# Splitting each weight load of an attention and channel-mix kernel into 120 and 8 partitions

## The chip, the cores and the metric

The kernel runs on one core of one Trainium2 chip. The metric is device time in microseconds (us): the median of 3 runs before the change was 168.54 us (168.08 to 169.32). The core has a matrix engine (TensorE, PE in the profile, with PEld for its weight loads), VectorE (DVE), ScalarE (ACT), GpSimd (POOL) and SyncE (SP). In this kernel SP issues nearly all transfers between the main memory (HBM) and the on-chip memory (SBUF, 128 partitions); the transfers themselves run on 16 DMA engines.

## The reference

The inputs are q, k and v (4 batches, 8 heads, 768 positions, head dimension 64) and the weights of a channel mix. All are float32.

```python
scores = scale * np.matmul(q, k.transpose(0, 1, 3, 2))
keep = is_sink | in_window        # first 4 positions, or the last 128
scores = np.where(keep, scores, -1000000000.0)
a = np.exp(scores - np.max(scores, axis=-1, keepdims=True))
a = a / (np.sum(a, axis=-1, keepdims=True) + 1e-09)
x = np.matmul(a, v)               # -> (4, 768, 512), heads side by side
...
x_prev = x shifted by one position
xk = mu_k * x + (1.0 - mu_k) * x_prev
xr = mu_r * x + (1.0 - mu_r) * x_prev
k = np.maximum(xk @ w_k, 0.0)     # w_k: 512 x 1024
v = k * k @ w_v                   # w_v: 1024 x 512
r = 1.0 / (1.0 + np.exp(-(xr @ w_r)))   # w_r: 512 x 512
out = r * v
```

## The kernel before

The work is cut into 12 units: four batches of three blocks of 256 positions. For each unit the kernel loads k, q and v, casts them to bfloat16, turns k and q so that the head dimension lies on the partitions (on TensorE, or with a transposing transfer in later units), forms the scores of the window and of the sinks, takes the exponential on ScalarE, masks on VectorE, multiplies with v on TensorE and divides (`attend`). `mix` then turns the result and forms xk and xr, and `ffn` does the three products with the weights. The `ffn` of a unit runs beside the attention of the next one.

Nothing is scheduled on the chip. Every step is an operation of a plan (`P.op`), and a list written out by hand, `ORDER`, gives the order in which the operations are emitted; `CHOICE` says which engine takes a step that several could do, `SLOTS` which buffer each tile gets. Negative entries of `ORDER` are matmuls on a tile of zeros (L1014) that keep TensorE running, most of them before real work is there. Each engine runs its own instructions in that order, and waits are set by the data and the buffers. The costs that stand in the calls of `P.op` (600.0, `service`, `descs`) are left from the search for the order and do nothing at run time.

The weights are loaded in five pieces of 1 MB each by `load_weight`: the two halves of w_k (`wka`, `wkb`), `wr`, and the two halves of w_v (`wva`, `wvb`). Each piece goes into one of three float32 buffers of the pool `w32` with 128 partitions of 4 x 512 values, that is four runs of 2 KB per partition. `cast` (L492 and on) then makes bfloat16 copies, on ScalarE (L498) or VectorE (L502, L504): `wk_sb`, `wr_sb`, `wv_h`. The pieces wva and wvb take the buffers of wka and wkb, so their transfers wait for the casts of those.

All these transfers are issued by SP, in the order of `ORDER`, between the loads of k, q and v (L304, L314, L334). Around the weights the order is: a v and a q load, wka, a k load, wkb, a k load, the two v loads of the second unit, one v load of the third, wr, wva, wvb, and then loads of the third and later units. Later SP also issues the transposing transfers (L559, L866) and the stores of the result (L1010, L921). The transfers take eight semaphores in turn, and the program has each issue on SP wait for the transfer that was issued eight before it.

The lines that the prediction names are L304, L314 and L334 (loads of v, k and q), L351 (loads of the weights), L498 and L502 (casts of the weights), L533, L540 and L643 (casts of k, q and v), L772 and L786 (exponential and mask), L805 (product with v), L885 (xk and xr), L950 (relu on VectorE) and L936 (product with w_k).

Of the kernel before, what the change touches and what calls it, by code (L numbers as in the profile page):

```python
# [183 lines left out]
def kernel(  # L184
# [29 lines left out]
    P = Plan()  # L214
# [27 lines left out]
    buf = P.buf  # L242
# [97 lines left out]
    def load_weight(what, rank):  # L340
        name, part = what[:2], what[2:]
        src = {"wk": moe_w_k, "wr": moe_w_r, "wv": moe_w_v}[name].rearrange(
            "(c p) f -> p c f", p=128)
        i = "ab".index(part) if part else 0
        if name == "wk":
            src = src[:, :, 512 * i:512 * i + 512]
        elif name == "wv":
            src = src[:, 4 * i:4 * i + 4]
        key = ("w32", name, i)
        queue, by = (nc.scalar, "ACT") if what in BY_ACT else (nc.sync, "SP")  # L350
        P.op(by, 600.0, lambda: queue.dma_start(out=buf[key], in_=src), rank,  # L351
             service=2930.0, descs=660, take=[("w32", key)], writes=[(name + "32", i)])

    for i, what in enumerate(LOADS):
        if what[0] == "w":
            load_weight(what, i - 100)
        elif what == "kq0":
            load(0, "kq", -100, 0, 4)
            if 0 in PAIRS:
                load(0, "kq", -99.5, 4, 8)  # L360
        else:
            load(int(what[-1]), what[:-1], i - 100)
# [7 lines left out]
    for i, src in enumerate((moe_mu_k, moe_mu_r)):  # L370
        P.op("ACT", 500.0, lambda i=i, src=src: nc.scalar.dma_start(
            out=rows8[NC * i:NC * i + NC, :], in_=src.rearrange("(c p) -> c p", p=128)), -100,
# [696 lines left out]
```

## Time and profile before

| What | Value |
|---|---|
| median of 3 runs | 168.54 us (168.08 to 169.32) |
| span of the profiled execution, first to last instruction | 167.6 us |
| TensorE, PE busy | 159.7 us, 95% |
| VectorE, DVE busy | 146.2 us, 87% |
| ScalarE, ACT busy | 133.4 us, 80% |
| GpSimd, POOL busy | 16.6 us, 10% |
| DMA moved | 34.60 MB, mean 206 GB/s |
| transfers of q, k and v | 24 each, 256 KB each |
| transfers of weights | 5, of 1 MB each |

The profile is of one execution; no time of its own is given for it beside its span, so the span stands 0.9 us below the median of the runs. A page of the profile lists busy times, the span in 40 slices, the DMA queues, the chain of work that ended last, and groups of instructions; further views give the instructions of a stretch in order of time, the waits between engines, and the share of time that the DMA engines were busy. That share can be over 1, since packets on an engine overlap. A line such as `43.86 0.43 DVE L533 CAST kb<-ks` is the start, the duration, the engine, the line of the kernel, the operation, and what it writes and reads. In brackets may stand how long the engine was idle before it and what ended that. PE's busy time holds matmuls on zeros too.

### The profile page before, as it was taken

The numbers are of one execution on the slowest core, as the hardware profiler recorded it, in microseconds if no ns is written. First come the engines' busy times: TensorE is split into PE (matmuls) and PEld (weight loads), VectorE is DVE, ScalarE is ACT, GpSimd is POOL, SyncE is SP. The second block draws the span as 40 slices with busy tenths as digits, with TensorE's granted clock in tenths as the row PEclk, the third lists the DMA queues.
The fourth block names the chain that finished last, engine by engine and source line by source line (L and its number), as shares of the span: only waits on it lengthen the run. The fifth ranks groups of instructions, "written<-read, shape, count | busy, mean of one in ns | idle before, by whom it ended". The sixth has DMA issues, their size and how long they took to land.

```text
span 167.6 us, 4210 instructions
## 1 busy us (share of the span) xinstructions
PE 159.7 (95%) x1601; PEld 102.4 (61%) x1601; DVE 146.2 (87%) x375; ACT 133.4 (80%) x221; POOL 16.6 (10%) x43
## 2 busy tenths in 40 slices
PE   6999997999999999899999999999999999999991
PEld 1447574755558576676556885665765576764850
DVE  5189999999999999899999999989798799998821
ACT  4269998999999997999879999989799829614340
POOL 6423021005000010022000000010010000000000
PEclk9999999999999999999999999999999999999999
DMA  4999989999899999979999999999997774131303
GB/s 102 300 327 369 346 172 312 372 324 328 189 248 166 204 294 224 253 153 133 218 256 149 214 239 174 233 219 200 211 189 185 194 162 155 63 66 63 125 0 125
DMA packets 79042, 34.60 MB, mean 206 GB/s; under 512 B 67112, under 2 KB 73520, under 8 KB 79024
## 3 DMA queue, kind: packets, MB, share of 16 engines
q1 hardware_dynamic: 79008, 34.35, 92.0%
q8 instruction: 12, 0.20, 0.5%
q14 instruction: 6, 0.05, 0.1%
q10 hardware_dynamic: 16, 0.00, 0.0%
HBM read 24.12 MB, written 6.29 MB: 181 GB/s over the span
## 4 chain that ended last, share of the span: by engine, by line
PE 58%; DVE 11%; DMA 11%; SPq 7%; ACT 7%; issue 3%; ACTq 0%; DVEq 0%
PE bank L936 18%; PE bank L994 18%; PE bank L976 8%; DMA vs<-in_v_dram 6%; SPq L334 5%; PE sc L718 4%; PE bank L805 4%; DMA qs<-in_q_dram 3%; ACT e L772 3%; DMA qt<-qb 2%; DVE ob L1003 2%; DVE e L786 2%; PE bank L846 2%; DVE x L822 2%; PE bank L573 2%
## 5 line engine op out<-in xcount | busy, mean ns | idle before, releaser
L936 PE MATMUL bank<-xk,wk_sb 128*128 128x256 bf16 x384 | 48.1, 273 | 0.1
L994 PE MATMUL bank<-wv_h,kk 128*128 128x512 bf16 x184 | 46.4, 379 | 0.0
L772 ACT ACTIVATE e<-sc 128x1024 bf16<-128x1024 f32 (+1 forms) x48 | 45.4, 974 | 1.2 <-PE sc L718 1.2
L936 PEld LDWEIGHTS <-wk_sb 128*128 128x128 bf16 x384 | 36.2, 98 | 7.6 <-issue 0.7
L786 DVE TENSOR_TENSOR e<-e,mask 128x1024 bf16<-128x1024 bf16 (+1 forms) x48 | 30.7, 655 | 0.7 <-ACT e L772 0.5
L946 ACT ACTIVATE rl<-bank 128x512 bf16<-128x512 f32 x38 | 22.4, 616 | 8.6 <-PE bank L936 8.5
L994 PEld LDWEIGHTS <-kk 128*128 128x128 bf16 x184 | 16.6, 98 | 14.4 <-issue 0.3
L976 PE MATMUL bank<-wr_sb,xr 128*128 128x512 bf16 x96 | 23.8, 379 | 0.0
L885 DVE SCALAR_TENSOR_TENSOR xr<-td,mu_all,xt 128x256 bf16<-128x256 bf16 x48 | 22.5, 482 | 0.0
L885 DVE SCALAR_TENSOR_TENSOR xk<-td,mu_all,xt 128x256 bf16<-128x256 bf16 x48 | 21.3, 477 | 0.1
L964 ACT ACTIVATE kk<-rl 128x512 bf16<-128x512 bf16 x26 | 16.7, 649 | 5.3 <-DVE rl L950 5.3
L822 DVE TENSOR_TENSOR x<-bank,rec 128x256 bf16<-128x256 f32 x48 | 19.2, 416 | 0.3
L1003 DVE SCALAR_TENSOR_TENSOR ob<-th,bank 128x512 f32<-128x512 f32 x23 | 15.7, 681 | 4.2 <-PE bank L994 3.3
L805 PEld LDWEIGHTS <-e 128*128 128x128 bf16 x352 | 14.4, 97 | 5.8 <-DVE e L786 1.0
L805 PE MATMUL bank<-vb,e 128*128 128x65 bf16 x352 | 16.9, 193 | 0.8 <-DVE e L786 0.8
L982 ACT ACTIVATE th<-bank 128x512 f32<-128x512 f32 x24 | 14.3, 616 | 3.6 <-PE bank L976 3.5
L1014 PE MATMUL bank<-warm 128*128 128x512 bf16 x44 | 13.8, 440 | 1.5 <-DVE warm L1032 1.1
L718 PE MATMUL sc<-qt,kt 64*128 64x128 bf16 (+1 forms) x256 | 13.9, 237 | 0.3 <-DMA qt<-qb 0.2
L976 PEld LDWEIGHTS <-xr 128*128 128x128 bf16 x96 | 8.9, 98 | 8.6
L718 PEld LDWEIGHTS <-kt 64*128 64x128 bf16 x256 | 9.3, 94 | 4.5 <-issue 3.0
L874 DVE TENSOR_TENSOR td<-xt 128x512 bf16<-128x512 bf16 x24 | 10.1, 425 | 0.8 <-ACT xt L855 0.8
L855 ACT COPY xt<-bank 128x512 bf16<-128x512 bf16 x15 | 9.1, 608 | 1.8 <-PE bank L846 1.8
(72 smaller groups left out, 157.9 us busy)
## 6 DMA issues: line engine op xcount, KB each, us to landing
vs<-in_v_dram SPq DMA_DIRECT2D x24, 256.0 KB, 5.0
ks<-in_k_dram SPq DMA_DIRECT2D x24, 256.0 KB, 5.6
qs<-in_q_dram SPq DMA_DIRECT2D x24, 256.0 KB, 5.1
out_dram<-ob SPq DMA_DIRECT2D x23, 256.0 KB, 2.9
w<-in_moe_w_k_dram SPq DMA_DIRECT2D x2, 1024.0 KB, 7.3
w<-in_moe_w_v_dram SPq DMA_DIRECT2D x2, 1024.0 KB, 8.6
w<-in_moe_w_r_dram SPq DMA_DIRECT2D x1, 1024.0 KB, 7.1
kt<-kb SPq DMA_TRANSPOSE x16, 4.1
```

The costliest lines, as they stand in the source:

```text
L718: nc.tensor.matmul(out=sc[:, a, o0:o1], lhsT=lhs[rows], rhs=rhs[rows], start=u not in BIAS, stop=True, skip_group_check=u in BIAS)
L772: nc.scalar.activation(out=buf[ek][:, :, lo:], in_=buf[sck][:, :, lo:], func=AF.Exp, scale=scale)
L786: nc.vector.tensor_tensor(out=at, in0=at, in1=m, op=ALU.mult)
L805: nc.tensor.matmul(out=o[:, g, a, :], lhsT=e[:, a, e0:e0 + 128], rhs=rhs, start=(T == 0 and i == 0), stop=(i == len(blocks) - 1), skip_gro ...
L822: P.op("DVE", dve(256), lambda ok=ok, rk=rk, c=c: nc.vector.tensor_tensor(out=buf["x", u][:, :, 128 * c:128 * c + 128].rearrange("p g (a d ...
L885: nc.vector.scalar_tensor_tensor(out=buf[key][:, c, :], in0=buf[tk][:, i, :], scalar=mu[w][:, c:c + 1], in1=xt[:, c, t0 - 1:t0 + 255], op0 ...
L936: nc.tensor.matmul(out=ps[:, i, :], lhsT=wk_sb[:, c, 128 * f:128 * f + 128], rhs=xk[:, c, :], start=(c == 0), stop=(c == NC - 1), skip_gro ...
L946: nc.scalar.activation(out=buf[rk], in_=buf[psk].rearrange("p (i t) -> p i t", i=2), func=AF.Relu)
L964: nc.scalar.activation(out=buf["kk", u][:, 2 * f2:2 * f2 + 2, :], in_=buf[rk], func=AF.Square)
L976: nc.tensor.matmul(out=buf[psk], lhsT=buf["xr", u][:, c, 128 * g:128 * g + 128], rhs=wr_sb[:, c, :], start=(c == 0), stop=(c == NC - 1))
L994: nc.tensor.matmul(out=buf[psk], rhs=wv_h[:, f, :], lhsT=buf["kk", u][:, f, 128 * g:128 * g + 128], start=(f == 0), stop=(f == NF - 1))
L1003: P.op("DVE", dve(512), lambda psk=psk, tk=tk, bk=bk: nc.vector.scalar_tensor_tensor(out=buf[bk], in0=buf[tk], scalar=1.0, in1=buf[psk], o ...
```

## The change

Each load of a weight piece, one transfer over 128 partitions before, becomes two transfers issued one behind the other: partitions 0 to 119, and partitions 120 to 127. They go to the same buffer and read the same bytes. No other transfer and no order is touched. SP issues five transfers more in all, and the casts wait for both parts of their piece.

```diff
         key = ("w32", name, i)
         queue, by = (nc.scalar, "ACT") if what in BY_ACT else (nc.sync, "SP")
-        P.op(by, 600.0, lambda: queue.dma_start(out=buf[key], in_=src), rank,
+        def rows():
+            for p0, p1 in ((0, 120), (120, 128)):
+                queue.dma_start(out=buf[key][p0:p1], in_=src[p0:p1])
+
+        P.op(by, 600.0, rows, rank,
              service=2930.0, descs=660, take=[("w32", key)], writes=[(name + "32", i)])
```

Lines below that place move by four; the prediction names the lines of before.

## The prediction

> **What bounds the kernel now.** I read the page first: the span, the slices, the DMA queues. All times are us from the span's start.
>
> ```profile
> span 167.6 us, 4210 instructions
> PE   6999997999999999899999999999999999999991
> DMA  4999989999899999979999999999997774131303
> q1 hardware_dynamic: 79008, 34.35, 92.0%
> q8 instruction: 12, 0.20, 0.5%
> q10 hardware_dynamic: 16, 0.00, 0.0%
> ```
>
> The reader is to see that TensorE (PE) and the DMA engines are both full from the second slice on (a slice is 4.2 us); the DMA digits fall only behind slice 30. The early PE digits are partly matmuls on a tile of zeros that keep it running. So I asked next who makes PE wait once real work has begun, by the waits of PE and by the stretches.
>
> ```profile
> PE bank L693 <- ACT rl L946: 0.6, 1, 0.6
> PE sc L718 <- DMA qt<-qb: 0.2, 1, 0.2
> ...
> 14.00:18.00 4.00, 3.92 (x52) 2.58 (x50) 3.81 (x13) 4.00 (x8) 1.57 (x2) 1.00 1.05 381
> 45.00:133.00 88.00, 86.88 (x952) 57.59 (x951) 81.90 (x212) 82.04 (x140) 4.69 (x11) 1.00 1.13 207
> ```
>
> The first two lines are all of PE's waits between 31 and 164, 0.8 in total. The last two are stretches (length, then PE, PEld, DVE, ACT and POOL busy, granted clock, DMA share, GB/s). From 31 on PE streams without a stop, at clock 1.00, so whatever makes it begin later there makes the end later by as much. What decides when it begins is the chain of waits between 12 and 31, together with VectorE's (DVE) and PE's timelines:
>
> ```profile
> 12.91 10.07 DMA vs<-in_v_dram
> 22.97 0.02 issue
> 23.00 0.43 DVE vb L643
> 23.43 1.19 DVE rl L950 x2
> 24.62 0.73 DVE xr L885
> 25.35 1.01 DVE e L786
> ...
> 21.66 1.29 DVE L786 TENSOR_TENSOR e<-e,mask 128x1024 bf16<-128x1024 bf16 x2
> 23.00 0.43 DVE L643 CAST vb<-vs 128x512 bf16<-128x512 f32 x1
> ...
> 26.42 0.42 PE L805 MATMUL bank<-vb,e 128*128 128x65 bf16 x8 [0.76 <-DVE e L786]
> ```
>
> A load of v issued at 12.91 lands at 22.98. DVE's previous instruction ends at 21.66 + 1.29 = 22.95 and its cast of that v starts at 23.00: DVE is full, and the load comes with no slack at all. The masks behind it feed PE, which already waits 0.76 for them at 26.42. A load that lands earlier buys nothing there; one that lands later costs PE its full lateness.
>
> **Why that load takes 10.07: it stands in a queue.** The issues and the rows for the loads of the weights:
>
> ```profile
> vs<-in_v_dram SPq DMA_DIRECT2D x24, 256.0 KB, 5.0
> ...
> 12.91 4.83 SPq L304 DMA_DIRECT2D vs<-in_v_dram  x2
> ...
> 13.78 8.13 SPq L304 DMA_DIRECT2D vs<-in_v_dram  x2
> 21.95 0.87 SPq L351 DMA_DIRECT2D w<-in_moe_w_r_dram  x1
> 22.93 4.39 SPq L351 DMA_DIRECT2D w<-in_moe_w_v_dram  x2
> ...
> L498 ACT ACTIVATE wk_sb<-w x4: 1107/1141/1181, 17.9 to 25.8; 128x1024 bf16<-128x1024 f32 x4
> L351 SPq DMA_DIRECT2D w<-in_moe_w_k_dram x2: 605/606/606, 9.5 to 11.6; - x2
> L351 SPq DMA_DIRECT2D w<-in_moe_w_v_dram x2: 367/400/434, 22.9 to 27.0; - x2
> L498 ACT ACTIVATE wv_h<-w x2: 1107/1126/1144, 33.7 to 36.5; 128x1024 bf16<-128x1024 f32 x2
> L502 DVE TENSOR_SCALAR wv_h<-w x2: 682/682/682, 35.4 to 37.1; 128x1024 bf16<-128x1024 f32 x2
> L351 SPq DMA_DIRECT2D w<-in_moe_w_r_dram x1: 867/867/867, 22.0 to 22.0; - x1
> L498 ACT ACTIVATE wr_sb<-w x1: 1070/1070/1070, 29.5 to 29.5; 128x1024 bf16<-128x1024 f32 x1
> DMA to landing us min/median/max: 7.1/7.6/9.2
> ...
> DMA to landing us min/median/max: 7.3/7.3/7.3
> ...
> DMA to landing us min/median/max: 7.9/7.9/7.9
> ...
> 22.00:24.00 2.00, 2.00 (x21) 1.67 (x18) 1.96 (x5) 2.00 (x4) 0.10 (x1) 1.00 0.76 170
> 24.00:26.00 2.00, 1.66 (x34) 1.13 (x32) 2.00 (x4) 2.00 (x5) 1.83 (x3) 1.00 0.90 215
> ```
>
> (The fence's w rows give issue to landing of all w loads: 7.1 is wr's and 9.2 the first wv half's. Then come those of the wk half issued at 9.5 and of the wv half issued at 27.0 alone, then two stretches.) The median v load lands in 5.0; this one needs twice that, and SP sits 8.13 on the issue of the next two (some 4 each, where 0.6 is usual). The engines, not SP, are the limit in this stretch, with about 5 us of work lined up. Both wk loads (issued at 9.5 and 11.6) stand ahead of this v in that line.
>
> **The change, part by part.** Each of the five loads (128 rows of 8 KB, 1 MB) becomes two transfers, of 120 and of 8 rows. No byte is added. What can cost is (a) how the rows spread over the 16 engines, (b) five more issues on SP, (c) the waits.
>
> (a) Price of a row. At 381 GB/s (the stretch 14 to 18, mostly wk) 1.049 MB takes 2.75; with 128 rows on 16 engines that is eight rows each, and a ninth on one engine costs 2.75 / 8 = 0.34. How do 120 and 8 rows spread? The nearest row of the trace is q10: two loads of four rows gave 16 packets in all, that is 2 × (4 rows + 4 completions): four rows went to four engines, one each. So I take the 8-row transfer as one row on each of eight engines. For 120 rows nothing here is a measure. The ends: 120 over 16 engines leaves some with seven, and the small transfer might fill just those, so nothing changes (0 per load); or only a power of two of engines is used (as with every 128, 64 and 4 rows in this trace), eight of them with 15 rows, and with one more 16 instead of eight, +2.75 per load. In between lie 15 engines with eight rows, eight of which get a ninth: +0.34. I take that, as it keeps eight rows per engine, which all loads of 128 rows have; both ends stay for the range. [...]
>
> First term: two wk loads ahead of the v load, 2 × 0.34 = 0.69. It lands at 23.66 instead of 22.97, DVE has nothing else to do (in-order, next in line is that cast), masks and PE follow: +0.69 on PE at 26.42.
>
> Second term: wr and the two wv loads add 3 × 0.34 = 1.03, in all 1.72 for what stands behind them, as long as the engines stay full. They do have a hole between 22 and 26 (shares 0.76 and 0.90), because wr's issue was held by SP's long v issue before it; that issue ends when the engines have made room, so the hole moves along with them and absorbs nothing. What comes just in time behind:
>
> ```profile
> 43.86 0.43 DVE L533 CAST kb<-ks 128x512 bf16<-128x512 f32 x1 [0.17 <-DMA ks<-in_k_dram]
> ...
> 48.73 0.87 DVE L885 SCALAR_TENSOR_TENSOR xk<-td,mu_all,xt 128x256 bf16<-128x256 bf16 x2
> ...
> 49.85 0.61 PE L936 MATMUL bank<-xk,wk_sb 128*128 128x256 bf16 x4
> ```
>
> DVE waits for this k load at 43.86, so it becomes 1.72 late; between there and the xk that ends at 49.60 it never idles, and PE uses xk at 49.85. PE is 0.69 late by then and has 0.25 cover: it waits 1.72 - 0.69 - 0.25 = 0.78. Behind that PE has no idle time to give back (0.8 in all). **Sum: 0.69 + 0.78 = 1.47.**
>
> (b) SP. Five issues, each priced as the one it doubles: 2 × 0.61 + 0.87 + 0.43 + 0.37 = 2.9, plus 0.04 between two. Two of them (1.3) push the v issue from 12.91 to about 14.2; it then stands in line 1.3 less, and SP's long issues behind it shrink instead. Two more fall into the wait that makes the 22.93 line 4.39 long (the second wv half goes into the buffer of the second wk half and waits for its last cast, 25.8 + 1.18). Cost 0 while the engines' line covers them; without cover all 3.1.
>
> (c) Waits. Each cast of a weight waits for both parts. Slack: wk 9.5 + 7.3 = 16.8 against 17.9, about 1; wr 22.0 + 7.1 = 29.1 against 29.5, 0.4, and the load gets later by 1.03, the cast by 0.69: 0.34 is still covered. First wv half 22.9 + 9.2 = 32.1 against 33.7, second 27.0 + 7.9 = 34.9 against 36.5, and DVE's casts of them start at 35.4 and 37.1. If a cast did wait, ScalarE's exps and copies behind it would wait too. The program also makes each SP issue wait for the transfer issued eight before it; with pairs, eight reach back over fewer bytes, but still some 5 us of engine work. Cost 0.
>
> The median of the three runs, 168.54, lies 0.9 above the profiled span of 167.6 (what lies around it). **168.54 + 1.47 = 170.0.**
>
> **The rivals.**
> - *Not slower: a late engine that has no ninth row.* A q8 packet holds 16 KB, and 12 of them take 0.5% of 16 × 167.6, 1.1 us each, on one engine while the others go on. A landing counts the last engine. If the late one is not among the eight that get more, their 0.69 vanishes beneath its 1.1, and at 43.86 only 1.72 - 1.1 = 0.6 is left, of which 0.25 is covered; if the engine spared is the late one, the DMA waits of DVE and ACT near 44 to 47 shrink (0.17 above). Time 168.0 to 169.0. [...] For: 10.07 is long even for a queue. Against: no view tells engines apart, and eight of 16 get more. [...]
> - *SP is the limit.* If SP's order, not the engines, sets the later loads, the 3.1 comes on top in part or whole: 170.7 to 173. For: everything the kernel loads, turns or stores goes through SP in one order, and five issues are added to it. Against: the 8.13 above is SP waiting for the engines, and a DMA share of 1.13 up to 133 says the same of the stretch behind.
> - *Doubling.* 120 rows on eight engines: +5.5 at the v load, +13.7 by 44: 174 to 182. For: only powers of two are in this trace. Against: an even split of 120 rows needs no power of two, and eight rows per engine is what all full loads here have.
> - *The change does nothing:* the program's SP list does have five transfers more, so this can only come as the first rival.
> - *Clearly faster* needs 1.7 of PE idle to go; behind 31 there is 0.8.
>
> **How the numbers follow.** My forecast's mechanism (169.1 to 170.8, about half on each side of 170.2) 0.46; late engine elsewhere 0.18; SP or a longer stream 0.20; doubling 0.09; shifted order that happens to gain 0.07. One per cent, 1.7, is about what a measurement of this kernel can tell from no change. Faster by over 1%: 0.07. Within: 0.18 and 0.25 of the forecast's 0.46, 0.43. Slower: the other 0.21, with 0.20 and 0.09, 0.50. Range: from 168.1, leaving out the gains, to 174.0, leaving out the doubling.
>
> **What would show it.** Right: the chain of waits has the v load landing 0.5 to 0.9 later after its cause, at 23.5 to 23.9, DVE idle in front of its vb cast, PE's wait for L786 1.3 to 1.6 instead of 0.76; issue to landing of the w parts about 7.5 to 8.5; DVE's kb cast near 45.5; no new wait of ACT for w. Wrong: the v load at 23.0 (late engine elsewhere), at 28 (doubling), or the loss first seen in SP's own waits behind 45. What would make it wrong most easily is that rows spread in some other way than eight and nine.

## The result and the profile after

The changed kernel takes **183.19 us** (median of 4 runs, 180.52 to 184.47) against 168.93 us for the kernel before (4 runs, 168.08 to 169.53): 1.0756 times the time, 95% interval 1.0645 to 1.0867. The ratio leaves out the runs of 183.38 and 184.47 us, which are more than 1.5% above the fastest of that kernel, and the profile below is of the first of these, with a mean granted clock of 0.953 where the two runs that count have 0.97. The forecast was 170.0 with a range of 168.1 to 174.0, so the change is slower as forecast, but by some nine times as much (0.0756 x 168.93 = 12.8 against 1.47), and the time lies outside the range.

The page of the kernel after, from the parts on busy time, slices and queues (all line numbers are four higher than before from the weight loads on):

```profile
span 181.4 us, 4223 instructions
...
PE 164.9 (91%) x1601; PEld 104.5 (58%) x1601; DVE 146.4 (81%) x375; ACT 134.1 (74%) x221; POOL 16.0 (9%) x43
...
PE   7899496968379999999999999999999999999991
...
PEclk9999858699859999999999999999999999999999
DMA  4999996999999899998799789999999685032303
...
q1 hardware_dynamic: 79043, 34.35, 86.3%
```

The damage lies in slices 5 to 12 (a slice is now 4.5 us): PE is idle there in part, and the clock granted to it falls. From slice 13 on PE is full again at full clock. The DMA engines are as busy as before. Of the 13.8 us by which this span is longer than the one before, PE's idle time is 8.6 (from 167.6 - 159.7 = 7.9 to 181.4 - 164.9 = 16.5) and PE's longer busy time for the same 1601 matmuls is 5.2.

The last row also bears on how the rows spread over the engines: 79043 packets against 79008 are 35 more, 7 for each of five loads, and all 35 are packets of 4 B (2636 against 2601 in the packet records). Such a packet is read as one completion for each engine that a transfer uses, as the prediction counted q10 (8 packets of 512 B and 8 of 4 B for its eight rows). With 15 engines for 120 rows and 8 for eight that is 15 + 8 - 16 = 7.

The stretches of the kernel after (length, then PE, PEld, DVE, ACT and POOL busy with their counts, granted clock, DMA share, GB/s); the first answers to the same stretch of before, which had 381 GB/s at a DMA share of 1.05:

```profile
14.00:18.00 4.00, 3.92 (x53) 2.56 (x51) 3.77 (x14) 3.80 (x6) 1.17 (x2) 1.00 1.07 215
18.00:22.00 4.00, 1.63 (x27) 1.09 (x26) 1.48 (x4) 1.65 (x3) 0.00 (x0) 0.88 1.01 182
22.00:26.00 4.00, 4.00 (x14) 1.86 (x14) 3.22 (x7) 2.50 (x4) 0.00 (x0) 0.50 1.07 196
...
16.00:60.00 44.00, 33.72 (x297) 20.07 (x294) 27.94 (x70) 28.93 (x45) 4.47 (x6) 0.81 1.01 216
60.00:120.00 60.00, 59.86 (x678) 40.70 (x675) 59.13 (x157) 56.98 (x97) 2.70 (x7) 1.00 1.01 208
```

Before, the stretch from 16 to 60 had:

```profile
16.00:60.00 44.00, 42.61 (x465) 27.73 (x462) 43.22 (x109) 42.98 (x72) 4.78 (x8) 1.00 1.09 267
```

This is the finding of the whole case: between 14 and 18, at the same share of busy engines, 215 GB/s instead of 381. The engines are not fewer (eight of sixteen would halve the share too); each byte takes longer on them. The packet records of the two traces (start, length and size of every packet) say so directly: a 2 KB packet of the two wk loads takes 161 ns in the mean after, and 91 ns before. The smaller packets of other loads are slower beside them too: those of 1 KB (q and k) between the first and the last wk packet take 88 ns instead of 50.

Where the lateness enters, in the timelines of VectorE, ScalarE and PE after (start, duration, engine, line, operation; in brackets the idle time before it and what ended it):

```profile
29.70 0.43 DVE L647 CAST vb<-vs 128x512 bf16<-128x512 f32 x1 [4.34 <-DMA vs<-in_v_dram]
50.33 0.43 DVE L647 CAST vb<-vs 128x512 bf16<-128x512 f32 x1 [4.23 <-DMA vs<-in_v_dram]
...
20.35 1.06 ACT L502 ACTIVATE wk_sb<-w 128x1024 bf16<-128x1024 f32 x1 [2.55 <-DMA w<-in_moe_w_k_dram]
28.50 1.06 ACT L502 ACTIVATE wk_sb<-w 128x1024 bf16<-128x1024 f32 x1 [4.00 <-DMA w<-in_moe_w_k_dram]
...
21.93 2.72 PE L1018 MATMUL bank<-warm 128*128 128x512 bf16 x6 [2.37 <-ACT xt L859]
29.62 1.05 PE L940 MATMUL bank<-xk,wk_sb 128*128 128x256 bf16 x8 [1.59 <-ACT wk_sb L502]
47.23 0.29 PE L764 MATMUL bank<-vsink,es 64*128 64x130 bf16 x4 [2.42 <-ACT th L986]
50.81 0.81 PE L809 MATMUL bank<-vb,e 128*128 128x65 bf16 x12 [2.08 <-DVE vb L647]
```

The cast of the v load that stands behind the two wk loads starts at 29.70 instead of 23.00: 6.7 late, where the forecast had 0.69. The casts of the weights now wait as well, by the list of waits:

```profile
ACT wk_sb L502 <- DMA w<-in_moe_w_k_dram: 6.5, 2, 4.0
...
ACT wv_h L502 <- DMA w<-in_moe_w_v_dram: 4.0, 2, 2.2
...
ACT wr_sb L502 <- DMA w<-in_moe_w_r_dram: 2.1, 1, 2.1
```

It is by one of these casts that the first batch of lateness reaches PE in this run. The first line is from the timeline of ScalarE before, the others are from the chain of the kernel after that ended last (start, duration, what):

```profile
21.91 1.16 ACT L498 ACTIVATE wk_sb<-w 128x1024 bf16<-128x1024 f32 x1
...
12.60 15.82 DMA w<-in_moe_w_k_dram
28.50 1.06 ACT wk_sb L502
...
34.27 16.03 DMA vs<-in_v_dram
50.33 0.44 DVE vb L647
```

The third wk cast starts at 28.50 instead of 21.91, 6.6 late and 1.2 ahead of the late v cast, and PE waits for it at 29.62. PE's gap of 2.37 before 21.93 is a wait for a copy (xt) that stands behind the first wk cast on ScalarE (20.35, before 17.90). The second batch comes by a later v load, issued behind wr and wv at 34.27 instead of 27.38; its cast is at 50.33 instead of 36.76.

### The profile page after: what moved, and what is told of

Its sections match the earlier page's. It is cut to its first block, busy times and chain, and to the rows that moved or that the text cites. A ratio compares the mean times of both kernels' runs of the same rounds, so it can differ in the third digit from the quotient of the medians.

```text
span 181.4 us, 4223 instructions
## 1 busy us (share of the span) xinstructions
PE 164.9 (91%) x1601; PEld 104.5 (58%) x1601; DVE 146.4 (81%) x375; ACT 134.1 (74%) x221; POOL 16.0 (9%) x43
## 3 DMA queue, kind: packets, MB, share of 16 engines
q1 hardware_dynamic: 79043, 34.35, 86.3%
## 4 chain that ended last, share of the span: by engine, by line
PE 66%; DMA 18%; SPq 6%; DVE 3%; ACT 2%; issue 1%; ACTq 0%
PE bank L998 21%; PE bank L940 19%; PE bank L980 10%; DMA vs<-in_v_dram 9%; DMA w<-in_moe_w_k_dram 9%; PE bank L809 6%; PE sc L722 4%; SPq L334 4%; SPq L353 2%; PE bank L850 2%; PE bank L764 1%; PE bank L577 1%; ACT wk_sb L502 1%; PE bank L910 1%; DVE ob L1007 1%
## 5 line engine op out<-in xcount | busy, mean ns | idle before, releaser
L940 PE MATMUL bank<-xk,wk_sb 128*128 128x256 bf16 x384 | 50.3, 279 | 3.2 <-ACT wk_sb L502 1.6
L998 PE MATMUL bank<-wv_h,kk 128*128 128x512 bf16 x184 | 47.3, 385 | 0.0
L940 PEld LDWEIGHTS <-wk_sb 128*128 128x128 bf16 x384 | 36.9, 100 | 12.4 <-issue 2.7
L980 PE MATMUL bank<-wr_sb,xr 128*128 128x512 bf16 x96 | 24.7, 390 | 0.0
L809 PE MATMUL bank<-vb,e 128*128 128x65 bf16 x352 | 18.1, 200 | 2.3 <-DVE vb L647 2.1
L809 PEld LDWEIGHTS <-e 128*128 128x128 bf16 x352 | 15.4, 101 | 7.4 <-issue 3.2
L647 DVE CAST vb<-vs 128x512 bf16<-128x512 f32 x9 | 3.8, 424 | 8.6 <-DMA vs<-in_v_dram 8.6
## 6 DMA issues: line engine op xcount, KB each, us to landing
w<-in_moe_w_v_dram SPq DMA_DIRECT2D x2, 960.0 KB, 13.8
```

The costliest lines, as they stand in the source:

```text
L809: nc.tensor.matmul(out=o[:, g, a, :], lhsT=e[:, a, e0:e0 + 128], rhs=rhs, start=(T == 0 and i == 0), stop=(i == len(blocks) - 1), skip_gro ...
L940: nc.tensor.matmul(out=ps[:, i, :], lhsT=wk_sb[:, c, 128 * f:128 * f + 128], rhs=xk[:, c, :], start=(c == 0), stop=(c == NC - 1), skip_gro ...
L980: nc.tensor.matmul(out=buf[psk], lhsT=buf["xr", u][:, c, 128 * g:128 * g + 128], rhs=wr_sb[:, c, :], start=(c == 0), stop=(c == NC - 1))
L998: nc.tensor.matmul(out=buf[psk], rhs=wv_h[:, f, :], lhsT=buf["kk", u][:, f, 128 * g:128 * g + 128], start=(f == 0), stop=(f == NF - 1))
```

## The experiments

Two theories were on the table once the trace had shown half the bytes at a full DMA share. **Ways** (theory A in the expectations): transfers that don't cover all 128 partitions are dealt to the engines in such a way that several engines write at once through the same way into SBUF, and each gets a part of it. **Pieces:** more and smaller transfers cost by themselves (issues on SP, completions, waits). The expectations add theory B, that such transfers use fewer engines (powers of two), and theory C, that the order of reading in HBM is slow. Times before that the ratios refer to are 169.2 to 169.3 us.

**1. The weight transfers alone** (label `loads_alone`). No computation: groups of four transfers of 2 KB runs, one group after the other, each waited for by VectorE.

```python
GROUPS = (0:128, 0:120, 0:112, 0:96, 0:64, 0:128:2, 64:128, 120:128, 0:32:4, 0:128:16, 0:8,
          0:120 other order in HBM, 0:128 other order, 0:120 of w_k, 0:128 of w_k,
          112:128, 0:120, 0:128)          # partitions written, as start:stop:step
for rows, src in GROUPS:
    for t in wide:                        # four tiles [128, 4, 512]
        nc.sync.dma_start(out=t[rows], in_=src[0:n])
    for t in reversed(wide):
        nc.vector.tensor_copy(out=seen[:, col:col + 1], in_=t[:, 0, 0:1])
```

> This kernel leaves all of the computation out: it loads parts of the weights into SBUF, in 18 groups of four equal transfers, and waits for each group (a copy of one column per buffer on VectorE) before the next begins. The groups differ in which partitions they fill: 0-127, 0-119, 0-111, 0-95, 0-63, every second, 64-127, 120-127, every fourth of 0-31, every sixteenth, 0-7, then 0-119 and 0-127 from another order of rows in HBM and from the wider weight, 112-127, and 0-119 and 0-127 once more. Theory A (the engines meet on shared ways into SBUF: 120 rows are dealt out so that several engines write into the same few partitions' way): the four loads of 0-119 move about 200 GB/s where 0-127 moves about 380, in whatever order the rows lie in HBM; and eight rows, one on each of eight engines, take up to four times as long into 120-127 or 0-7 as into every fourth of 0-31. Theory B (fewer engines, by powers of two): 0-119 at half rate, and so 0-95 and 0-111; eight rows take the same time wherever they go. Theory C (the order of reading in HBM): 0-119 is slow only from the order that the kernel uses, and fast where each partition reads one run of 8 KB.

VectorE's timeline in that run; the bracket is the time of one group of four, in the order above (0:112, 0:64, 0:128:2, 120:128, 0:32:4 and, last, 0:120 and 0:128 once more are shown, after the first 0:120):

```profile
40.13 0.34 DVE L52 COPY seen<-wide 128x1 f32<-128x1 f32 x4 [21.69 <-DMA wide<-in_moe_w_r_dram]
54.59 0.34 DVE L52 COPY seen<-wide 128x1 f32<-128x1 f32 x4 [14.12 <-DMA wide<-in_moe_w_r_dram]
...
83.36 0.34 DVE L52 COPY seen<-wide 128x1 f32<-128x1 f32 x4 [12.90 <-DMA wide<-in_moe_w_r_dram]
91.75 0.34 DVE L52 COPY seen<-wide 128x1 f32<-128x1 f32 x4 [8.05 <-DMA wide<-in_moe_w_r_dram]
...
111.04 0.34 DVE L52 COPY seen<-wide 128x1 f32<-128x1 f32 x4 [6.14 <-DMA wide<-in_moe_w_r_dram]
116.22 0.34 DVE L52 COPY seen<-wide 128x1 f32<-128x1 f32 x4 [4.85 <-DMA wide<-in_moe_w_r_dram]
...
226.53 0.34 DVE L52 COPY seen<-wide 128x1 f32<-128x1 f32 x4 [21.45 <-DMA wide<-in_moe_w_r_dram]
240.16 0.34 DVE L52 COPY seen<-wide 128x1 f32<-128x1 f32 x4 [13.29 <-DMA wide<-in_moe_w_r_dram]
```

120 rows take 21.45, 128 rows 13.29: fewer bytes in 1.6 times the time. 64 neighbouring rows take 12.90, the same number on every second partition 8.05. 0:96, not shown, takes 15.20, longer than 128 rows; 120:128 takes 6.14 and 0:32:4 4.85, so eight rows do not take the same time wherever they go, which theory B expected. The rates inside four of these groups (0:64, 0:128:2, and the last 0:120 and 0:128), in the stretches of the same run (length, VectorE's busy time, clock, DMA share, GB/s):

```profile
72.00:82.00 10.00, 0.00 (x0) 1.00 1.01 207
85.00:90.00 5.00, 0.00 (x0) 1.00 0.96 334
...
208.00:224.00 16.00, 0.00 (x0) 1.00 1.00 203
229.00:238.00 9.00, 0.00 (x0) 1.00 1.05 392
```

So the loss is there with no other work on the chip. It does not come from the reading side: with the rows in another order in HBM, 0:120 still took 20.91 and 0:128 12.39, and from w_k 22.02 and 13.60; and 0:64 and 0:128:2 read the very same bytes at different rates. Theory C falls. Nor are engines missing: the run's 24240 packets on q1 are those of its rows and stores and one completion per engine, if 120 rows use 15 engines, eight rows 8 and all other groups 16.

The packet records of this run show what is slow: the median 2 KB packet takes 84 ns in 0:128 and 0:128:2, 165 to 166 in 0:120 and 0:64, 109 in 0:112 and 136 in 0:96.

**2. The ways, with packets twice as long** (label `loads_alone2`). The first set left one group open: 0:128:16 took 4.83, as 0:32:4 did, but so little that the issues could have been its limit. The same program with runs of 4 KB and groups of few rows:

```diff
-GROUPS = (...)
+GROUPS = (0:128, 120:128, 0:32:4, 0:128:16, 0:64:8, 0:8, 0:4, 0:16:4, 0:128:32,
+          0 and 32, 0 and 64, 0 and 1, 0 and 4, 0:120)
```

> All computation is left out, as in the first kernel of loads alone; 14 groups of four transfers with runs of 4 KB, to see which partitions share a way. If a way is four neighbouring partitions and the four 32 above them (0-3 with 32-35), and 64 and up has ways of its own: with one row per engine, a packet takes one unit into 0:32:4, two into every sixteenth and into 0:64:8 (two rows per way), four into 120-127, 0-7 and 0-3, one into 0:16:4, two into 0, 32, 64, 96 and into 0 and 32, one into 0 and 64, two into 0 and 1, one into 0 and 4. If a way is eight neighbouring partitions: eight units into 120-127 and 0-7, and 0 and 4 share.

VectorE's timeline again, the groups from 120:128 on, without 0:64:8 (7.54), and to 0 and 4:

```profile
41.34 0.34 DVE L48 COPY seen<-wide 128x1 f32<-128x1 f32 x4 [11.29 <-DMA wide<-in_moe_w_k_dram]
47.59 0.34 DVE L48 COPY seen<-wide 128x1 f32<-128x1 f32 x4 [5.91 <-DMA wide<-in_moe_w_k_dram]
55.59 0.34 DVE L48 COPY seen<-wide 128x1 f32<-128x1 f32 x4 [7.66 <-DMA wide<-in_moe_w_k_dram]
...
74.80 0.34 DVE L48 COPY seen<-wide 128x1 f32<-128x1 f32 x4 [11.00 <-DMA wide<-in_moe_w_k_dram]
86.05 0.34 DVE L48 COPY seen<-wide 128x1 f32<-128x1 f32 x4 [10.91 <-DMA wide<-in_moe_w_k_dram]
91.88 0.34 DVE L48 COPY seen<-wide 128x1 f32<-128x1 f32 x4 [5.50 <-DMA wide<-in_moe_w_k_dram]
99.17 0.33 DVE L48 COPY seen<-wide 128x1 f32<-128x1 f32 x4 [6.95 <-DMA wide<-in_moe_w_k_dram]
106.61 0.34 DVE L48 COPY seen<-wide 128x1 f32<-128x1 f32 x4 [7.10 <-DMA wide<-in_moe_w_k_dram]
112.62 0.34 DVE L48 COPY seen<-wide 128x1 f32<-128x1 f32 x4 [5.67 <-DMA wide<-in_moe_w_k_dram]
119.67 0.33 DVE L48 COPY seen<-wide 128x1 f32<-128x1 f32 x4 [6.72 <-DMA wide<-in_moe_w_k_dram]
125.72 0.33 DVE L48 COPY seen<-wide 128x1 f32<-128x1 f32 x4 [5.71 <-DMA wide<-in_moe_w_k_dram]
```

Each row goes to an engine of its own here (as the four rows of q10 in the profile before did, and the run's 8460 packets on q1 come out so), so each engine moves the same 16 packets of 4 KB in every group, and still there are three steps of time. 5.5 to 5.9: 0:32:4, 0:16:4, 0 and 64, 0 and 4. 6.7 to 7.7: 0:128:16, 0:128:32, 0 and 32, 0 and 1. 10.9 to 11.3: eight or four neighbouring rows. In the packet records of this run the median 4 KB packet takes 159 ns in the groups of the first step, 296 to 332 in the second and 596 to 605 in the third: one, two and four times as long. The pairs show which partitions share a way: 0 and 1 disturb each other (6.72), 0 and 4 don't (5.71); 0 and 32 do (7.10), 0 and 64 don't (5.67). All groups of up to eight rows of this run agree with ways of four neighbouring partitions and the four that lie 32 above them; one, two or four engines on a way are then the three steps. Carried on to the partitions that were not tried, an estimate, this map has 16 ways in all, of which 0:64 has eight and 0:128:2 all sixteen; the first set has 207 and 334 GB/s there.

The map alone does not say why 120 rows are slow, for by it they reach all 16 ways; the author's explanation is which engine gets which rows, and no view tells engines apart. The 392 GB/s of 0:128, with 84 ns to a packet, are taken as engines that don't meet. The 203 GB/s of 0:120, half of it, is what two engines to a way on average would give, by the step from 159 ns to between 296 and 332 above, and so is its median packet of 165 to 166 ns against 84. That its engines meet on the ways is inferred from this; by which rule the rows are dealt, of 120 or of 128, no run shows.

**3. The same bytes in two pieces of 128 partitions** (label `runs_split`).

```diff
-            for p0, p1 in ((0, 120), (120, 128)):
-                queue.dma_start(out=buf[key][p0:p1], in_=src[p0:p1])
+            for c in (0, 2):
+                queue.dma_start(out=buf[key][:, c:c + 2, :], in_=src[:, c:c + 2, :])
```

> Each weight load is two transfers again, five issues more on SyncE and two waits in each cast, but both have all 128 partitions (two of the four runs of 2 KB each). If the issues and waits cost something, it shows here: up to 3.1 us over before (172). If the loss is in the rows (theories A and B), the time is that of before within 1 us: 168 to 170.

168.65 us, ratio 1.000 (0.9956 to 1.0044). The v load's cast starts at 22.73. Five more issues, more completions and casts that wait for two parts cost nothing when the pieces cover all partitions. The theory of pieces falls.

**4. Two halves, lower and upper** (label `p64`), **and every second partition** (label `even_odd`).

```diff
-            for p0, p1 in ((0, 120), (120, 128)):
+            for p0, p1 in ((0, 64), (64, 128)):                        # p64
...
+            for w in range(2):                                         # even_odd
+                queue.dma_start(out=buf[key][w::2], in_=src[w::2])
```

> Two transfers of 64 partitions each, 0-63 and 64-127: four rows on each of 16 engines. Theory B (too few engines) has 16 engines here and expects the time of before, 168 to 170. Theory A: half of the partitions have half of the ways, 16 engines on them, so each part runs at up to half rate and the loss is like that of the change, 178 to 186; unless the two parts overlap, which would make it less.

> Two transfers of 64 partitions each again, with 16 engines and four rows on each as in p64 (179.8), but the even partitions and the odd ones instead of the lower and the upper half. Shared ways (theory A): 0::2 alone ran at 84 ns a packet, 0-63 at 166, so the loss of p64 goes away: 168 to 170, ratio 0.99 to 1.01. If it were the number of rows or of partitions of a transfer that is slow, it stays at 178 to 182.

p64 takes 179.83 us, ratio 1.0643 (1.0573 to 1.0712); even_odd 170.07, just over the time expected, ratio 1.005 (1.0001 to 1.0099). Both are two transfers of 64 rows, of the same bytes, on 16 engines each (both have 79088 packets on q1, 5 x 16 more than before); only the partitions that go together differ. Which partitions a transfer writes is thus enough for a loss of 6%.

**5. 112 and 16 rows** (label `p112`): as p64, with `((0, 112), (112, 128))`.

> Two transfers of 112 and 16 partitions: seven rows and one row on each of 16 engines, so no engine has more than eight rows. Theory B (engines) and the ninth row both expect the time of before, 168 to 170. Theory A expects a loss wherever seven rows in a row per engine meet on one way: 172 to 184.

177.2 us, ratio 1.0469 (1.0376 to 1.0563). Both pieces use all 16 engines (79088 packets again), so the loss needs no idle engine, and theory B falls here as in p64. Its size is not what the groups alone give: four of 0:112 took 14.12, hardly more than 0:128, and four of 112:128 6.32, yet the v load's cast starts at 28.19, 5.2 late. In this kernel the wk packets take 150 ns in the mean, where the two groups alone, mixed as seven to one, give 125; and 1 KB packets of q and k among them take 86 ns instead of 50 before. An estimate from these, (150 - 91) x 1024 / 16 for the wk packets and (86 - 50) x 628 / 16 for the others, is 5.2 us per engine, what the v load is late. Why 112 rows are slower beside other loads than alone stays open.

**6. Only some of the loads** (label `wk_only`, the pair of transfers for the two wk loads alone; label `no_wk`, for wr and the two wv alone).

```diff
-            for p0, p1 in ((0, 120), (120, 128)):
+            for p0, p1 in ((0, 120), (120, 128)) if name == "wk" else ((0, 128),):   # wk_only
```

> Only the two wk loads are split into 120 and 8 partitions. By the loads alone, 120 rows take 5.0 us instead of 3.1 and eight rows 1.0 more, 2.9 per load: the v load behind them, which VectorE awaits at 23.0, is 5.8 late and the matrix engine with it, and its clock falls in the gap: 174 to 178. If the later three loads carried the loss, it would be 168 to 171.

> Only wr and the two wv loads are split, three of the five. 8.7 us more of engine time behind the v load at 23; casts of wv and the loads at 36 to 47 come late by that, less the cover of 0.3 to 1.6 before them: 174 to 178. If the time before 30 carried nearly all of the loss, 168 to 171.

wk_only 175.29 us, ratio 1.0346 (1.0284 to 1.0408); no_wk 176.82, ratio 1.0453 (1.0389 to 1.0516). From VectorE's timeline and PE's, first of wk_only:

```profile
29.04 0.43 DVE L647 CAST vb<-vs 128x512 bf16<-128x512 f32 x1 [2.97 <-DMA vs<-in_v_dram]
...
22.65 0.81 PE L1018 MATMUL bank<-warm 128*128 128x512 bf16 x3 [2.68 <-ACT xt L859]
```

then of the kernel before (the first line) and of no_wk:

```profile
36.76 0.42 DVE L643 CAST vb<-vs 128x512 bf16<-128x512 f32 x1
...
42.59 0.43 DVE L647 CAST vb<-vs 128x512 bf16<-128x512 f32 x1 [4.44 <-DMA vs<-in_v_dram]
...
43.07 0.52 PE L809 MATMUL bank<-vb,e 128*128 128x65 bf16 x12 [2.56 <-DVE vb L647]
```

Each group of loads delays the v load that stands behind it, the wk loads the one whose cast was at 23.00 before, wr and wv the one at 36.76 (42.59 here), and the two losses nearly add up: 0.0346 + 0.0453 = 0.080 against 0.0756 for both.

**7. How much the small piece costs** (labels `eight_extra` and `eight_extra_spread`). The kernel before, each load whole, with an extra transfer of eight rows and three quarters of their length behind it, into a tile that nothing reads: eight neighbouring partitions, or every fourth of a stretch of 32.

```diff
+    pool("spare", 1, [128, 3, 512], FP32)
...
+            queue.dma_start(out=buf[key], in_=src)
+            queue.dma_start(out=P.pools["spare"][0][next(spares)], in_=src[120:128, 0:3])
```

> The kernel before, each weight load whole (128 partitions), and behind it an extra transfer of eight rows of three runs of 2 KB (48 KB) into eight neighbouring partitions of a tile that nothing reads: the small piece alone, without the loss of the large one. In the loads alone, four pieces into 120 to 127 took 6.14 and four into 0:32:4 4.85; in the second set (twice the bytes) 11.29 and 5.91, so (11.29 - 5.91) / 16 = 0.34 us more per packet of 4 KB, about 0.17 per packet of 2 KB, on top of 0.08. Three packets are then 0.75 on each of eight engines; two wk pieces stand ahead of the v load. If the small piece carries its share of the loss: the v load lands about 1.5 later (24.2 to 24.8), the time is 170.5 to 173. If the loss lies in the 120 rows alone: within 1% of 169, as the same piece spread out.

> The same extra eight rows of 48 KB per weight load, into every fourth partition of a stretch of 32 instead of eight neighbouring ones. By shared ways: three packets of 0.08 = 0.25 per piece on eight engines, 0.5 at the v load at most, time 168.5 to 170. If an extra small transfer costs by itself, whatever its partitions: the same as the other kernel.

171.07 us, ratio 1.0116 (1.0071 to 1.0162), and 169.47, ratio 0.9999 (0.9956 to 1.0042). The v load's cast starts at 23.95, 0.95 later than before, and at 23.21. The expected 24.2 to 24.8 was a little too much, the order of the two was as expected: the extra small transfer was free with its rows on every fourth partition (0.9999), which by the map have ways of their own, and cost 1.2% on neighbouring ones, where four of its engines share one. As an estimate, at full length that would be some 0.0116 x 4 / 3 = 0.015 of the 0.0756: about a fifth of the loss would be the piece of eight rows, the rest the piece of 120.

## Why the prediction was wrong

- *What bounds the kernel* was right: PE streams behind 31, the DMA engines are full ahead of it, and the v load behind the two wk loads comes without slack. In wk_only its cast (29.04) is where the chain that ended last enters; in the kernel after, a wk cast (28.50) is ahead of it. The second batch was placed at a k load (43.86 before); VectorE's wait there is for a v load that the prediction did not look at (50.33 instead of 36.76, and PE behind it at 50.81). wk_only and no_wk show the two batches apart.
- **(a), the price of a row, is the step that failed.** Fifteen engines with eight rows and eight with a ninth was an estimate of the author's; the count agrees with it (35 packets more), and which rows an engine gets no run shows. But a row was priced the same wherever it goes, 2.75 / 8 = 0.34. The group times give (21.45 - 13.29) / 4 = 2.0 more for each piece of 120, and 0.95 / 2 x 4 / 3 = 0.6 for each piece of eight, together 2.7 per load and 5.4 at the v load, of the 6.7 measured there. The packet records of the kernel itself give 4.5 for the wk packets, (161 - 91) x 1024 / 16, and 1.5 for the slower q and k packets among them, (88 - 50) x 628 / 16: 6.0 of the 6.7, an estimate. So the price of a row had to hold both how fast an engine is on its way into SBUF, and what it does to its neighbours. "Nothing here is a measure" for 120 rows was said, but the bounds were set on how many engines are used, and none on how fast an engine is.
- *Doubling* was the rival nearest in size, 174 to 182 against 183.19, and with a forecast of the v load at 28 (29.70). That it came so near is luck, for its reason was not the right one: eight engines would have shown a halved DMA share, and the share is 1.07 at 215 GB/s.
- *(b) SP at nothing* holds: runs_split has the same five issues more and takes 1.000 times the time.
- *(c) the waits at nothing* is the second step that failed, by following (a): the slack it read (1 us before a wk cast, 0.4 before wr's) was to cover 0.69. With the loads late by several us, ScalarE waits 6.5 + 4.0 + 2.1 for weights, the third wk cast is 6.6 late, and it, not the v load, is on the chain that ended last.
- **A term was missing: the clock of PE.** The forecast counted lateness as PE's idle time alone. Between 16 and 60 the granted clock is 0.81 instead of 1.00, and PE is busy 5.2 longer over the span, of the 13.8 by which the profiled run is longer. The 0.50 sets in at 21, within the gap of 2.37 that ends at 21.93, and from 60 on the clock is 1.00. That gaps are what lowers it was not tested apart, and eight_extra_spread speaks against a simple rule (below).
- *Late engine*, *SP is the limit* and *clearly faster* did not occur. No run shows an engine that lags behind the rest as a rule; the v load's cast came 6.7 later (29.70), where that rival had the load at 23.0. The chance of 0.50 for slower was right in sign. The 0.09 for doubling was low for a rival that hung on the rate of 120 rows, of which the prediction said that nothing was a measure.

## What to carry to other kernels

In these runs the rate of a load hung on which partitions it wrote, not only on its bytes and its number of engines (64 rows on 16 engines: 207 GB/s into 0:64, 334 into 0:128:2). By that, one would first try to keep large loads at 128 partitions and, where one has to be cut, to cut it along the free dimension (1.000 here) or by every second partition (1.005) rather than into neighbouring blocks (1.05 to 1.08). A DMA share that stayed full while GB/s fell (1.07 at 215 instead of 1.05 at 381), with packets of the same size, pointed to engines that share a way here; with other packets it need not (the kernel before has a share of 1.13 at 207 GB/s between 45 and 133, behind all loads of weights). Where a load feeds the matrix engine with no slack, look at the granted clock behind it too: here PE was busy 5.2 us longer for the same matmuls, at 0.81 between 16 and 60.

## What was not expected of the hardware

- Four engines on one way, by the map: four transfers of eight neighbouring rows take 11.3 where the same bytes on every fourth partition take 5.9, and four rows (10.9) are as slow as eight.
- 120 rows take 1.6 times as long as 128 (21.45 against 13.29), and in the kernel after, the 1 KB packets of other loads beside them are slower (88 ns instead of 50).
- In eight_extra_spread the granted clock dips (0.50 between 28 and 30); the longest wait that PE had between 18 and 60 in its timeline was 0.76, at 26.64. The kernel before has a wait of 0.76 at 26.42, and no dip. From the page of eight_extra_spread:

```profile
span 168.2 us, 4215 instructions
...
PEclk9999997899999999999999999999999999999999
```

The span is 0.6 above that of before, so this dip cost little, but here the clock fell without a gap of some 2 us ahead of it. What decides it is not shown.
